# First layers of the last two tiles by Strassen's seven products, and one shared stage of second layers, in a retention and two feed-forward networks

## The chip, the cores and the metric

One core of a Trainium2 chip. The metric is the device time of one execution, in microseconds (us). TensorE (PE) multiplies matrices and adds up in PSUM, which has eight banks of 128x512 f32; VectorE (DVE), ScalarE (ACT) and GpSimd (POOL) do elementwise work; SyncE (SP) issues most DMAs. Each engine takes its instructions in the order in which they are written.

## The reference

```python
for t in range(S):
    state = gamma[None, :, None, None] * state + np.einsum('bhd,bhe->bhde', k[:, :, t], v[:, :, t])
    y[:, :, t] = scale * np.einsum('bhd,bhde->bhe', q[:, :, t], state)
...
h = x @ w_in
g = np.where(pos, h, np.where(neg, 0.0, (h + beta) ** 2 / (4.0 * beta)))
y1 = g @ w_out
...
a = x @ w1
b = x @ w2
h = a * b @ w3
return (h @ w_out).astype(np.float32)
```

Retention over 4 batches, 8 heads, 768 positions of 64; then the first network on 3072 tokens (512 to 2048 to 512), and the second (512 to 1024 twice, multiplied, to 1024, to 512). All inputs and outputs are f32.

## The kernel before

The 768 positions are cut in six chunks of 128 (c), so the tokens in six tiles (i) of 512. An f32 matrix is kept as two parts, a hi and the rest lo, and each product is three matmuls (hi hi, lo hi, hi lo): `split` makes the parts, hi by a cast on ACT, lo by a subtraction on DVE. Weights come from DRAM as raw words and pass a conversion of two ACT and four DVE operations (`convert`).

**The first network and the retention** are written by a planner. Its PE order is written by hand (the list `pe`), and the other engines' orders follow from costs and due times. `qk_ops` and `pv_ops` are the two attention pieces of a batch and chunk, with banks called pe or pa. `h_ops[i, f]` is a first layer's block f of 16 for tile i (bank hps, 12 matmuls), followed by Relu and Square on ACT and a max and min on DVE; `y_ops[i, f]` is the second layer's block f (banks y1acc, four at once, 12 matmuls). For tiles under LATE (0, 1 and 2) the first layers come ahead, beside the attention, and wait in DRAM (g_d). The last tile's blocks are written out by hand behind the plan, and beside them the weights of the second network are prepared: `prepare_ab` makes the seven operands of a unit and stores them in wab_d.

**The second network.** First w3 and the last matrix are multiplied together (`emit_w3o`, steps u = 0 to 15; `fetch_w3` reads blocks, `load_w3` splits one a step ahead; banks w3acc, result wc). Then come three pairs of tiles. A pair has eight units (f), and `emit_ab` does one: seven products of six matmuls in the order p1, p2, p6, p5, p7, p3, p4 (Strassen's scheme in its Winograd form), on the banks bank_a, bank_c and bank_b, of which ACT makes copies c. The eight sums c1 and c2 are multiplied elementwise to p and q. Between products stand output blocks of the unit before (`out_blocks`, oacc; four with three matmuls each). Behind the eighth unit come the output blocks of f = 6 and f = 7 for the first tile of the pair, the evacuation of their four banks (ost, ACT and DVE in turn), and a pass of 96 matmuls for the second tile in the same banks. The operands of the next pair (yop, seven for each half kb) are made of four sums t (`add_y`) and a split each (`split_y`), for kb = 0 in unit 6 and between the output blocks, for kb = 1 in the second tile's pass.

```python
                if more and f == 6:
                    add_y(i + 1, 0)
                    for _ in range(2):
                        split_y(*ahead.pop(0))
                    fetch_y1(i + 1, 1, range(2))
```

Units 0 to 7 come from wab_d or are made on the spot (unit 7), and later ones are read by `load_unit` two units ahead, 1792 KB each.

## Time and profile before

| | us |
|---|---|
| median of 3 runs (lowest, highest) | 1040.75 (1040.54, 1041.38) |
| profiled execution | 1037.49 |
| its span in the trace | 1035.7 |
| PE busy | 1016.9 |
| DVE busy | 566.1 |
| ACT busy | 437.5 |
| POOL busy | 93.1 |

The span runs from the first to the last instruction of the one profiled execution; its own time has 1.8 us more around it. Mean granted TensorE clock 0.998. Matmuls overlap, so the mean duration of one is longer than the step to the next one's start. In a timeline row the bracket tells how long the engine was idle before, and what ended it.

### The profile page before, as it was taken

What the parts mean: (1) busy time and instruction counts of PE and PEld (TensorE: products, weight loads), DVE (VectorE), ACT (ScalarE), POOL (GpSimd) and SP (SyncE); (2) the same over time, 40 slices, a digit from 0 to 9 for tenths busy, and PEclk for the clock granted to TensorE, in tenths of its full rate; (3) what the DMA queues carried; (4) which work ended last, traced back from release to release, by engine and by line L of the source; (5) the groups of instructions that cost most, each with busy time, mean ns of one, the idle gap of its engine ahead of it and who ended that gap; (6) DMA issues with size and microseconds to landing.
All of it is one profiled execution on the core that took longest, in us unless ns stands there. A gap on an engine that the chain in (4) does not pass through costs nothing.

```text
span 1035.7 us, 14337 instructions
## 1 busy us (share of the span) xinstructions
PE 1016.9 (98%) x5492; PEld 828.8 (80%) x5492; DVE 566.1 (55%) x847; ACT 437.5 (42%) x719; POOL 93.1 (9%) x121
## 2 busy tenths in 40 slices
PE   7799999999999999999999999999999999999998
PEld 5688878887788888888888887888878888888886
DVE  5988378724445666666536676633482434624340
ACT  3477457632233454455435555432341323322320
POOL 1212422211200001000000010000000000000000
PEclk9999999999999999999999999999999999999999
DMA  9997749939689977867638996344372435434402
GB/s 297 232 251 220 271 143 366 364 131 369 230 326 393 354 284 259 295 238 295 217 152 312 340 408 217 138 143 175 134 259 89 165 143 193 163 132 142 148 30 77
DMA packets 77384, 235.51 MB, mean 227 GB/s; under 512 B 9474, under 2 KB 9858, under 8 KB 71428
## 3 DMA queue, kind: packets, MB, share of 16 engines
q1 hardware_dynamic: 68576, 198.74, 54.9%
q0 software_dynamic: 8448, 35.66, 9.1%
q8 instruction: 43, 0.70, 0.3%
q10 hardware_dynamic: 292, 0.20, 0.1%
q14 instruction: 25, 0.20, 0.1%
HBM read 175.84 MB, written 58.72 MB: 226 GB/s over the span
## 4 chain that ended last, share of the span: by engine, by line
PE 86%; DMA 5%; issue 4%; DVE 2%; ACT 2%; POOL 0%; SPq 0%; DVEq 0%; POOLq 0%; ACTq 0%
PE bank_a L782 12%; PE y1acc L273 8%; PE y1acc L275 7%; PE y1acc L274 7%; PE hps L273 7%; PE hps L275 7%; PE hps L274 7%; PE bank_b L782 6%; PE oacc L823 4%; PE oacc L824 4%; PE oacc L825 4%; PE bank_c L782 3%; PE pa L513 2%; PE w3acc L275 1%; PE w3acc L274 1%
## 5 line engine op out<-in xcount | busy, mean ns | idle before, releaser
L273 PE MATMUL hps<-xh,win 128*128 128x512 f32 x384 | 152.0, 396 | 2.2 <-ACT xh L529 1.8
L273 PE MATMUL y1acc<-g,wo 128*128 128x512 f32 x384 | 151.6, 395 | 1.4 <-ACT g L269 1.4
L275 PE MATMUL hps<-xl,win 128*128 128x512 f32 x384 | 150.2, 391 | 0.0
L274 PE MATMUL hps<-xh,win 128*128 128x512 f32 x384 | 150.1, 391 | 0.0
L275 PE MATMUL y1acc<-g,wo 128*128 128x512 f32 x384 | 149.6, 390 | 0.0
L274 PE MATMUL y1acc<-g,wo 128*128 128x512 f32 x384 | 149.6, 390 | 0.0
L782 PE MATMUL bank_a<-yop,unit 128*128 128x512 f32 x576 | 146.0, 390 | 0.7 <-ACT c L797 0.6
L782 PEld LDWEIGHTS bank_a<-yop,unit 128*128 128x128 f32 x576 | 107.9, 188 | 24.0 <-ACT c L797 1.6
L587 ACT ACTIVATE r<-hps 128x512 f32<-128x512 f32 x81 | 48.4, 597 | 122.8 <-PE hps L275 119.4
L590 DVE SCALAR_TENSOR_TENSOR r<-hps,r 128x512 f32<-128x512 f32 x81 | 55.7, 688 | 81.2 <-ACT r L589 79.8
L273 PEld LDWEIGHTS hps<-xh,win 128*128 128x128 f32 x384 | 72.5, 189 | 19.9 <-ACT xh L529 2.3
L273 PEld LDWEIGHTS y1acc<-g,wo 128*128 128x128 f32 x384 | 72.0, 188 | 19.0 <-ACT g L269 1.8
L809 DVE TENSOR_TENSOR c<-bank_b,c 128x512 f32<-128x512 f32 x24 | 16.6, 692 | 128.0 <-PE bank_b L782 128.0
L275 PEld LDWEIGHTS hps<-xl,win 128*128 128x128 f32 x384 | 72.4, 188 | 16.1 <-DVE xl L530 0.9
L275 PEld LDWEIGHTS y1acc<-g,wo 128*128 128x128 f32 x384 | 72.1, 188 | 15.6 <-DVE g L270 0.4
L274 PEld LDWEIGHTS hps<-xh,win 128*128 128x128 f32 x384 | 72.5, 189 | 14.5
L274 PEld LDWEIGHTS y1acc<-g,wo 128*128 128x128 f32 x384 | 72.1, 188 | 14.4
L782 PE MATMUL bank_b<-yop,unit 128*128 128x512 f32 x288 | 73.1, 389 | 0.0
L782 PEld LDWEIGHTS bank_b<-yop,unit 128*128 128x128 f32 x288 | 54.1, 188 | 11.3
L589 ACT ACTIVATE r<-r 128x512 f32<-128x512 f32 x81 | 51.2, 632 | 2.6
L269 ACT CAST p<-c 128x512 fp32r<-128x512 f32 x24 | 14.9, 622 | 84.3 <-DVE c L814 84.3
L329 DVE TENSOR_TENSOR g<-g 128x512 fp32r<-128x512 f32 x48 | 33.1, 699 | 31.2 <-ACT g L327 31.2
(173 smaller groups left out, 1587.3 us busy)
## 6 DMA issues: line engine op xcount, KB each, us to landing
wo<-wo_d SPq DMA_DIRECT2D x80, 512.0 KB, 6.6
unit<-wab_d SPq DMA_DIRECT2D x23, 1024.0 KB, 4.8
unit<-wab_d SPq DMA_DIRECT2D x23, 768.0 KB, 4.2
g_d<-r POOLq DMA_DIRECT2D x48, 256.0 KB, 4.0
g<-g_d SPq DMA_DIRECT2D x48, 256.0 KB, 6.2
wo_d<-wo POOLq DMA_DIRECT2D x16, 512.0 KB, 6.0
raw<-in_w_dram SPq DMA_DIRECT2D x16, 512.0 KB, 6.7
raw<-in_w3t_dram SPq DMA_DIRECT2D x8, 1024.0 KB, 7.1
```

The costliest lines, as they stand in the source:

```text
L273: nc.tensor.matmul(out=ps, lhsT=lh, rhs=rh, start=first, stop=False)
L274: nc.tensor.matmul(out=ps, lhsT=ll, rhs=rh, start=False, stop=False)
L275: nc.tensor.matmul(out=ps, lhsT=lh, rhs=rl, start=False, stop=last)
L329: return plan.op("DVE", 0.7, lambda: nc.vector.tensor_tensor(out=dst.ap[:, 1, :], in0=at(), in1=dst.ap[:, 0, :], op=ALU.subtract), r=[src, ...
L513: nc.tensor.matmul(out=ps2.ap[64 * e:64 * e + 64, h, j * C:(j + 1) * C], lhsT=v_t[:, 2 * p + h, :] if own else old.ap[r, p, :], rhs=a_t[:, ...
L587: plan.op("ACT", 0.6, lambda: nc.scalar.activation(out=r.ap, in_=ps.ap, func=AF.Relu, bias=0.5, scale=0.5), r=[ps], w=[r])
L589: plan.op("ACT", 0.63, lambda: nc.scalar.activation(out=r.ap, in_=r.ap, func=AF.Square), w=[r])
L590: plan.op("DVE", 0.7, lambda: nc.vector.scalar_tensor_tensor(out=r.ap, in0=ps.ap, scalar=1.0, in1=r.ap, op0=ALU.max, op1=ALU.min), r=[ps], ...
L782: nc.tensor.matmul(out=ps, lhsT=x, rhs=z, start=first and kb + k == 0, stop=kb == 1 and k == 2, skip_group_check=True,)
L823: nc.tensor.matmul(out=ps, lhsT=lh, rhs=wh, start=(f == 0), stop=False)
L824: nc.tensor.matmul(out=ps, lhsT=lh, rhs=wl, start=False, stop=False)
L825: nc.tensor.matmul(out=ps, lhsT=ll, rhs=wh, start=False, stop=(f == NF2 - 1))
```

## The change

1. Tiles 4 and 5 (PAIR) do their first layers as the second network does its own: `plan_hu(n)` makes blocks 2n and 2n+1 for both tiles in seven products, on one bank h and the two banks of pa, with operands made by `plan_unit` and `plan_x_pair`. For the weights of it, the converted w_in blocks are stored in DRAM (win_d) behind their conversion, two of them from their parts by POOL (`keep_win`).
2. LATE is 4: tiles 0 to 3 have their g in DRAM. Tiles 3 and 2 share one stage of second layers: tile 3 takes two banks of h and the two of pa, tile 2 the four of acc, and each weight block is loaded once. Second layers of tile 4 lie between Strassen products, those of tile 5 end the plan; nothing is written by hand behind it.
3. Retention of chunks 4 and 5 lies beside the first layers of tile 3 and second layers of tile 1; `h_ops[0, 1]` stands ahead of `kv_ops[0]`, the mask's two multiplications are exchanged.
4. The second network's unit weights aren't prepared ahead. `prepare_unit` makes each of the 24 units from one 512 KB read: ACT and DVE split, POOL makes the four sums. w_out2 is converted in the plan's last stage, with one block of w3 (DIRECT).
5. `add_y` and all seven `split_y` of kb = 0 stand behind the eighth unit.

```diff
-LATE = 3
-EARLY_AB = 7
+LATE = 4
+PAIR = 4
+KEEP = 260.0
+DIRECT = 1
+FEW = 3
...
+            if n == 2:
+                d = win_kept[f] = win_kept[f + 1] = Val(None, None)
+                plan.op("SP", 0.45, lambda: nc.sync.dma_start(out=win_d[f // 2], in_=u.ap.bitcast(F32)),
+                        r=[u], w=[d], size=512)
...
+        if c >= PAIR:
+            for kb in range(2):
+                if (c, kb) not in xs:
+                    xs[c, kb] = Val("w", lambda: wpool.tile([P, 2, 512], F32, tag="w", name="xs"))
+                plan.op("ACT", 0.45, lambda kb=kb: nc.scalar.copy(
+                    out=xs[c, kb].ap[:, :, b * C:b * C + C], in_=got()[:, :, kb]), r=[ps2], part=[xs[c, kb]])
+        else:
+            split_x(b, c, ps2, got)
...
+    SUMS = ((3, 2, 3, ALU.add), (2, 0, 2, ALU.subtract), (0, 3, 0, ALU.subtract), (1, 1, 0, ALU.subtract))
...
+    def plan_unit(n):
+
+        u = Val("u", lambda: cpool.tile([P, 1024], F32, tag="u", name="u"))
+        uh = Val("xh", lambda: xpool.tile([P, NK, TT], F32R, tag="xh", name="unit"))
+        ul = Val("xl", lambda: xpool.tile([P, NK, TT], F32R, tag="xl", name="unit"))
+        plan.op("SP", 0.45, lambda: nc.sync.dma_start(out=u.ap, in_=win_d[n]),
+                r=[win_kept[2 * n], win_kept[2 * n + 1]], w=[u], size=512)
+
+        def halves(v, hi, lo, a, b):
+            done = Val(None, None)
+            plan.op("ACT", 0.18 + 0.00088 * (b - a), lambda: nc.scalar.copy(out=hi(), in_=u.ap[:, a:b]),
+                    r=[u], part=[v, done])
+            plan.op("DVE", 0.15 + 0.00106 * (b - a), lambda: nc.vector.tensor_tensor(
+                out=lo(), in0=u.ap[:, a:b], in1=hi(), op=ALU.subtract), r=[u, done], part=[v])
+
+        halves(uh, lambda: uh.ap[:, 0], lambda: uh.ap[:, 1], 0, 512)
+        halves(ul, lambda: ul.ap[:, 2, 0:256], lambda: ul.ap[:, 2, 256:512], 768, 1024)
+        for o, x, y, op in SUMS:
+            plan.op("DVE", 0.43, lambda o=o, x=x, y=y, op=op: nc.vector.tensor_tensor(
+                out=block(u.ap, o), in0=block(u.ap, x), in1=block(u.ap, y), op=op), w=[u])
+        halves(uh, lambda: uh.ap[:, 2], lambda: uh.ap[:, 3], 0, 512)
+        halves(ul, lambda: ul.ap[:, 0], lambda: ul.ap[:, 1], 512, 1024)
+        return uh, ul
...
+    def plan_hu(n):
+        uh, ul = plan_unit(n)
+        bank = Val("h", lambda: ps_h.tile([P, TT], F32, tag="h", name="bank"))
+        pair = Val("pa", lambda: psum["a"].tile([P, 2, 512], F32, tag="pa", name="banks"))
+        at = {"a": lambda: bank.ap, "x": lambda: pair.ap[:, 0], "y": lambda: pair.ap[:, 1]}
+        ops = hu_ops[n] = []
+
+        def product(name, where, first):
+            def fn():
+                w = views((uh.ap, ul.ap))[name]
+                for kb in range(2):
+                    x = xops[kb, name].ap
+                    lh, ll, rh, rl = w[:, 0, kb, :], w[:, 1, kb, :], x[:, 0, :], x[:, 1, :]
+                    for k, (l, r) in enumerate(((lh, rh), (ll, rh), (lh, rl))):
+                        nc.tensor.matmul(
+                            out=at[where](), lhsT=l, rhs=r, start=first and kb + k == 0,
+                            stop=kb == 1 and k == 2, skip_group_check=True,
+                        )
+
+            ops.append(plan.op("PE", 1.362, fn, r=[uh, ul, xops[0, name], xops[1, name]],
+                               w=[bank if where == "a" else pair]))
+
+        def copy(where):
+            c = Val("st", lambda: new_st("c"))
+            plan.op("ACT", 0.6, lambda: nc.scalar.copy(out=c.ap, in_=at[where]()),
+                    r=[bank if where == "a" else pair], w=[c])
+            return c
+
+        def gate(f, src, src_at, second):
...
+        product("p1", "a", True)
+        c1 = copy("a")
+        product("p2", "x", True)
+        plan.op("DVE", 0.7, lambda: nc.vector.tensor_tensor(
+            out=c1.ap, in0=pair.ap[:, 0], in1=c1.ap, op=ALU.add), r=[pair], w=[c1])
+        gate(2 * n, c1, lambda: c1.ap, False)
+        product("p6", "a", False)
+        c2 = copy("a")
+        product("p5", "y", True)
+        c5 = copy("y")
+        product("p7", "a", False)
+        c3 = copy("a")
+        product("p3", "y", False)
+        plan.op("DVE", 0.7, lambda: nc.vector.tensor_tensor(
+            out=c2.ap, in0=pair.ap[:, 1], in1=c2.ap, op=ALU.add), r=[pair], w=[c2])
+        gate(2 * n, c2, lambda: c2.ap, True)
+        plan.op("DVE", 0.7, lambda: nc.vector.tensor_tensor(
+            out=c3.ap, in0=c3.ap, in1=c5.ap, op=ALU.add), r=[c5], w=[c3])
+        gate(2 * n + 1, c3, lambda: c3.ap, True)
+        product("p4", "a", False)
+        gate(2 * n + 1, bank, lambda: bank.ap, False)
...
+        hs = [Val("h", lambda: ps_h.tile([P, TT], F32, tag="h", name="y1acc")) for _ in range(2)]
+        pair = Val("pa", lambda: psum["a"].tile([P, 2, 512], F32, tag="pa", name="y1acc"))
+        return [*((v, lambda v=v: v.ap) for v in hs), *((pair, lambda j=j: pair.ap[:, j]) for j in range(2))]
...
+        for n, i in enumerate(tiles):
+            if f == 0:
+                banks[i] = y_banks(i, n < len(tiles) - 1)
+            if i == PAIR + 1:
+                g = Val("wo", lambda: new_wo("g"))
+                plan_split(g, g_last[f // 2], (slice(None), f % 2))
+            else:
+                g, _ = gs.pop((i, f))
...
+    def load_unit(n):
+        u = wpool.tile([P, 1024], F32, tag="w", name="unit_w")
+        nc.sync.dma_start(out=u, in_=spill[("wab", n % NF2)])
+        arrived[("unit", n)] = u
+
+    def prepare_unit(n):
+
+        u = arrived.pop(("unit", n))
+        a, b = units_ahead = unit_tiles()
+        split(a[:, 0], a[:, 1], u[:, 0:512])
+        split(b[:, 2, 0:256], b[:, 2, 256:512], block(u, 3))
+        yield
+        for o, x, y, op in SUMS:
+            nc.gpsimd.tensor_tensor(out=block(u, o), in0=block(u, x), in1=block(u, y), op=op)
+        yield
+        split(a[:, 2], a[:, 3], u[:, 0:512])
+        yield
+        split(b[:, 0], b[:, 1], u[:, 512:1024])
+        units[n] = views(units_ahead)
...
-        pe += [h_ops[0, 0], kv_ops[0], qk_ops[0, 1], qk_ops[1, 1], pv_ops[0, 1], qk_ops[2, 1], pv_ops[1, 1],
-               h_ops[0, 1], qk_ops[3, 1], pv_ops[2, 1], pv_ops[3, 1]]
+        pe += [h_ops[0, 0], h_ops[0, 1], kv_ops[0], qk_ops[0, 1], qk_ops[1, 1], pv_ops[0, 1], qk_ops[2, 1],
+               pv_ops[1, 1], qk_ops[3, 1], pv_ops[2, 1], pv_ops[3, 1]]
...
+            if f < 10:
+                pe.append(y_ops[1, f + 4])
+                if f in (5, 9):
+                    pe.append(pieces.pop(0))
+        assert not pieces
+        pe += [y_ops[1, NF1 - 2], y_ops[1, NF1 - 1]]
...
+        few_jobs = len(pe)
+        lagging = [y_ops[2, NF1 - 2], y_ops[2, NF1 - 1], *(y_ops[PAIR, f] for f in range(NF1))]
+        for n in range(NF1 // 2):
+            for j, o in enumerate(hu_ops[n]):
+                pe.append(o)
+                if j in (1, 3):
+                    pe.append(lagging.pop(0))
+        end_jobs = len(pe)
+        pe += [y_ops[PAIR, NF1 - 2], y_ops[PAIR, NF1 - 1]]
+        last_jobs = len(pe)
+        pe += [y_ops[PAIR + 1, f] for f in range(NF1)]
...
+        raws = [(load_rows(w_out2[j], w_out2[j + 1]), finish_wo2(j), None) for j in range(0, NF2, 2)]
+        direct = [Val("wo", lambda: wpool.tile([P, 2, 512], F32, tag="wo", name="w3f", bufs=10)) for _ in range(DIRECT)]
+        for j in range(DIRECT):
+            raws.append((load_rows(w3t[j]), lambda u: None, direct[j]))
...
+        fetches = [u for h in range(2) for u in range(NF2 * h + DIRECT, NF2 * h + NF2)]
+        for n in range(0, len(fetches), 2):
+            fetch_w3(fetches[n:n + 2])
+            if n == 2:
+                fetch_y1(0, 0, range(4))
+        load_w3(0)
...
+            if u == 2 * NF2 - 2:
+                for _ in prepare_unit(0):
+                    pass
...
+        n_units = NF2 * (NTILE // 2)
         for i in range(NTILE // 2):
             more = i + 1 < NTILE // 2
-            ahead = y_of(i + 1)
             for f in range(NF2):
-                n = 8 * i + f
-                steps = prepare_ab(n + 1) if EARLY_AB <= n + 1 < NF2 else ()
+                n = NF2 * i + f
+                if 0 < n < n_units - 1:
+                    load_unit(n + 1)
+                steps = prepare_unit(n + 1) if n + 1 < n_units else iter(())
                 emit_ab(i, f, out_blocks(f - 1) if 0 < f < NF2 - 1 else (), steps)
-                if not EARLY_AB <= n + 2 < NF2 and n + 2 < 8 * (NTILE // 2):
-                    load_unit(n + 2)
-                if n + 4 in range(EARLY_AB, NF2):
-                    fetch_ab(n + 4)
+                for _ in steps:
+                    pass
                 if more and f == 5:
                     fetch_y1(i + 1, 0, range(4))
-                if more and f == 6:
-                    add_y(i + 1, 0)
-                    for _ in range(2):
-                        split_y(*ahead.pop(0))
-                    fetch_y1(i + 1, 1, range(2))
+            ahead = y_of(i + 1)
+            if more:
+                add_y(i + 1, 0)
             for x in out_blocks(NF2 - 2):
                 emit_out(*x)
             if more:
                 while ahead[0][1] == 0:
                     split_y(*ahead.pop(0))
-                fetch_y1(i + 1, 1, range(2, 4))
+                fetch_y1(i + 1, 1, range(4))
             for x in out_blocks(NF2 - 1):
                 emit_out(*x)
                 evac_out(2 * i, x[3], x[0])
```

**ACT at the join of two pairs.** Before: from the first copy of unit 7's bank_a to the copies (ost) of the first tile's banks; f_ and t__ are inputs and sums for yop.

```order
L797 COPY c_6556<-bank_a 128x512
L802 COPY c_6557<-bank_a 128x512
L804 COPY c_6559<-bank_b 128x512
L807 COPY c_6558<-bank_a 128x512
L269 CAST p<-c_6556 128x512
L269 CAST q<-c_6557 128x512
L269 CAST yop<-t__6537 128x512 x2
L269 CAST yop<-t__6538 128x512
L269 CAST yop<-f_6431 128x512
L269 CAST yop<-t__6538 128x512
L628 COPY ost<-oacc 128x512 x2
```

After, from unit 7's copy of bank_b on:

```order
L968 COPY c_6644<-bank_b 128x512
L971 COPY c_6643<-bank_a 128x512
L273 CAST unit<-unit_w 128x512 x2
L273 CAST p<-c_6641 128x512
L273 CAST q<-c_6642 128x512
L273 CAST yop<-f_6536 128x512
L273 CAST yop<-f_6540 128x512
L273 CAST yop<-t__6716 128x512 x2
L273 CAST yop<-t__6717 128x512
L273 CAST yop<-f_6542 128x512
L273 CAST yop<-t__6717 128x512
L832 COPY ost<-oacc 128x512 x2
```

Two casts of the next unit stand ahead of p and q, and all seven yop casts stand between q and the ost copies. Before there are five, and the two from f_ stood ahead of unit 7's first copy.

**DVE at the same join.** Before, from c1's multiplication of unit 7 on:

```order
L814 TENSOR_TENSOR c_6556<-bank_a,c_6556 128x512
L270 TENSOR_TENSOR p<-c_6556,p 128x512
L270 TENSOR_TENSOR q<-c_6557,q 128x512
L270 TENSOR_TENSOR yop<-t__6537,yop 128x512 x2
L270 TENSOR_TENSOR yop<-t__6538,yop 128x512
L270 TENSOR_TENSOR yop<-f_6431,yop 128x512
L270 TENSOR_TENSOR yop<-t__6538,yop 128x512
L630 COPY ost<-oacc 128x512 x2
```

After, from the same multiplication on, with the unit's subtraction ahead of it:

```order
L274 TENSOR_TENSOR unit<-unit_w,unit 128x512
L978 TENSOR_TENSOR c_6641<-bank_a,c_6641 128x512
L274 TENSOR_TENSOR unit<-unit_w,unit 128x512
L274 TENSOR_TENSOR p<-c_6641,p 128x512
L274 TENSOR_TENSOR q<-c_6642,q 128x512
L923 TENSOR_TENSOR t__6716<-f_6538,f_6536 128x512
L924 TENSOR_TENSOR t__6717<-f_6542,f_6538 128x512
L925 TENSOR_TENSOR t__6716<-f_6542,t__6716 128x512
L926 TENSOR_TENSOR t__6717<-f_6540,t__6716 128x512
L274 TENSOR_TENSOR yop<-f_6536,yop 128x512
L274 TENSOR_TENSOR yop<-f_6540,yop 128x512
L274 TENSOR_TENSOR yop<-t__6716,yop 128x512 x2
L274 TENSOR_TENSOR yop<-t__6717,yop 128x512
```

The four sums t have moved from unit 6 to behind q, ahead of the first yop subtraction.

**SP at the end of the second layers.** y_d is y1 in DRAM. Before, around the four stores of the last tile:

```order
L644 DMA f_5568<-y_d_82 128x512
L661 DMA w3f<-sp_w_4_202 128x512
L661 DMA w3f<-sp_w_5_203 128x512
L1023 DMA y_d_86<-y1st 128x512 x4
L661 DMA w3f<-sp_w_6_204 128x512
L661 DMA w3f<-sp_w_7_205 128x512
L644 DMA f_5748<-y_d_81 128x512
```

After:

```order
L800 DMA wo<-wo_d_102 128x1024
L365 DMA raw<-in_w3t_dram 128x2048
L839 DMA y_d_86<-y1st 128x512 x4
L857 DMA w3f<-sp_w_1_202 128x512
L857 DMA w3f<-sp_w_2_203 128x512
L857 DMA w3f<-sp_w_3_204 128x512
L857 DMA w3f<-sp_w_4_205 128x512
```

Each fetch serves one of the 16 steps u; before, those of the first 14 stand ahead of the four stores (the last two of them are shown), after, none does, and a raw read of w3's block 0 has their place.

**ACT at the second network's first unit.** Before, at the end of the w3 product:

```order
L269 CAST w3s<-w3f 128x512
L269 CAST yop<-f_5754 128x512
L269 CAST wc<-w3acc 128x512 x4
L269 CAST yop<-t__5805 128x512
L797 COPY c_5956<-bank_a 128x512
```

After:

```order
L273 CAST w3s<-w3f 128x512
L273 CAST yop<-f_5785 128x512
L273 CAST unit<-unit_w 128x512
L273 CAST unit<-unit_w 128x256
L273 CAST unit<-unit_w 128x512 x2
L273 CAST wc<-w3acc 128x512 x4
L273 CAST yop<-t__5836 128x512
L961 COPY c_5997<-bank_a 128x512
```

Four casts of unit 0 stand ahead of the four wc casts, and so ahead of c1's copy of bank_a.

## Rows read from the trace of the kernel before

**Rows 1.** The page's parts 1 and 2: busy time; PE in 40 slices.

```profile
PE 1016.9 (98%) x5492; PEld 828.8 (80%) x5492; DVE 566.1 (55%) x847; ACT 437.5 (42%) x719; POOL 93.1 (9%) x121
...
PE   7799999999999999999999999999999999999998
```

**Rows 2.** The page's part 5, a costly group: busy us, mean ns, idle before.

```profile
L273 PE MATMUL hps<-xh,win 128*128 128x512 f32 x384 | 152.0, 396 | 2.2 <-ACT xh L529 1.8
```

**Rows 3.** The chain that ended last, 600 to 680 us: start, us, what.

```profile
670.13 1.36 PE bank_a L782 x6
```

**Rows 4.** Waits of PE: waited for, us in total, times, longest us.

```profile
PE pe L513 <- DVE qk L482: 3.2, 1, 3.2
PE pe L513 <- DVE a L472: 2.5, 3, 1.5
...
PE pe L513 <- DVE sbd L537: 1.5, 1, 1.5
PE y1acc L273 <- ACT g L269: 1.4, 1, 1.4
PE bank_a L782 <- ACT c L797: 0.6, 1, 0.6
PE pe L513 <- DVE q L482: 0.5, 1, 0.5
PE oacc L823 <- ACT ost L628: 0.4, 2, 0.2
```

**Rows 5.** Windows of PE: us, busy (instructions), granted clock, DMA share, GB/s.

```profile
43.00:44.00 1.00, 1.00 (x15) 0.70 1.10 289
44.00:46.00 2.00, 2.00 (x5) 0.50 1.05 170
46.00:47.00 1.00, 1.00 (x4) 0.59 1.09 256
```

**Rows 6.** Timeline, end of the second layers: start, us, engine, line, operation.

```profile
623.33 0.50 PE L273 MATMUL y1acc<-g,wo 128*128 128x512 f32 x1 [1.38 <-ACT g L269]
...
626.43 2.46 SPq L1023 DMA_DIRECT2D y_d<-y1st  x4
626.45 0.39 PE L273 MATMUL w3acc<-wo,w3s 128*128 128x512 f32 x1
```

**Rows 7.** DMAs issued from 620 to 700 us: KB each, median us to landing.

```profile
f<-y_d SPq DMA_DIRECT2D x5, 256.0 KB, 2.7
...
w3f<-sp_w SPq DMA_DIRECT2D x4, 256.0 KB, 6.0
```

**Rows 8.** Timeline, first unit of the second network.

```profile
668.13 2.63 ACT L269 CAST wc<-w3acc 128x512 fp32r<-128x512 f32 x4 [2.26 <-PE w3acc L275]
...
671.53 0.59 ACT L797 COPY c<-bank_a 128x512 f32<-128x512 f32 x1 [0.25 <-PE bank_a L782]
```

**Rows 9.** POOL's groups: busy us, mean ns, idle before.

```profile
L482 POOL TENSOR_TENSOR q<-q,decay 128x512 f32<-128x512 f32 x16 | 22.2, 1385 | 204.4 <-PE pa L460 148.7 <-issue 53.6 <-PE pe L460 1.6
```

**Rows 10.** Timeline, first join of two pairs.

```profile
763.46 0.39 PE L823 MATMUL oacc<-wc,p 128*128 128x512 f32 x1
...
764.30 0.68 DVE L814 TENSOR_TENSOR c<-bank_a,c 128x512 f32<-128x512 f32 x1
...
765.02 0.62 ACT L269 CAST p<-c 128x512 fp32r<-128x512 f32 x1 [3.49 <-DVE c L814]
...
766.06 1.14 ACT L269 CAST yop<-t__6537 128x512 fp32r<-128x512 f32 x2
...
766.88 1.28 DVE L270 TENSOR_TENSOR yop<-t__6537,yop 128x512 fp32r<-128x512 f32 x2
...
768.67 1.10 ACT L628 COPY ost<-oacc 128x512 f32<-128x512 f32 x2
...
769.30 0.50 PE L823 MATMUL oacc<-wc,q 128*128 128x512 f32 x1 [0.20 <-ACT ost L628]
...
770.61 21.77 SPq L844 DMA_DIRECT2D out_dram<-ost  x8
```

More of the change, by code (lines that the diff above doesn't have):

```diff
@@ L261, in retention_then_two_ffns @@
     decay = const.tile([P, NP, C], F32, name="decay")
-    block = const.tile([P, NP, D], F32, name="block")
+    span = const.tile([P, NP, D], F32, name="span")
     small = const.tile([P, H + C], F32, name="small")
@@ L301, in convert @@
         for n, (cost, fn) in enumerate(load):
-            plan.op("SP", cost, lambda fn=fn: fn(raw.ap), part=[raw], size=s * 512 / len(load) * (1.6 if len(load) == 4 else 1.0), bound=bound, after=after)
+            plan.op("SP", cost, lambda fn=fn: fn(raw.ap), part=[raw], size=s * 512 / len(load) * (1.6 if len(load) == 4 else 1.0),
+                    bound=bound, after=after).floor = floor
         odd = lambda: raw.ap[:, 1::2]
@@ L335, in retention_then_two_ffns @@
     wo_kept = [None] * NF1
+    win_d = [dram.tile([P, 1024], F32, name=f"win_d{n}") for n in range(NF1 // 2)]
+    win_kept = {}
     def load_win(f, n):
@@ L537, in update @@
                 plan.op("DVE", 0.43, lambda: nc.vector.tensor_tensor(
-                    out=new.ap, in0=at(), in1=block, op=ALU.mult), r=[kv, blocks], w=[new])
+                    out=new.ap, in0=at(), in1=span, op=ALU.mult), r=[kv, blocks], w=[new])
             else:
@@ L543, in update @@
                 plan.op("DVE", 0.43, lambda: nc.vector.tensor_tensor(
-                    out=new.ap, in0=t.ap, in1=block, op=ALU.mult), r=[t, blocks], w=[new])
+                    out=new.ap, in0=t.ap, in1=span, op=ALU.mult), r=[t, blocks], w=[new])
             sbd[b] = new
@@ new lines, in keep_win @@
+    def keep_win(f, after, bound):
+        t, w = Val("st", lambda: new_st("win")), win[f]
+        d = win_kept[f] = Val(None, None)
+        plan.op("POOL", 1.36, lambda: nc.gpsimd.tensor_tensor(
+            out=t.ap, in0=w.ap[:, 0, :].bitcast(F32), in1=w.ap[:, 1, :].bitcast(F32), op=ALU.add),
+            r=[w], w=[t], after=after, bound=bound).floor = bound - 20.0
+        plan.op("POOL", 0.6, lambda: nc.gpsimd.dma_start(
+            out=win_d[f // 2][:, 512 * (f % 2):512 * (f % 2) + 512], in_=t.ap), r=[t], w=[d], size=256).floor = bound - 18.0
@@ new lines, in unit_tiles, with views @@
+    def unit_tiles():
+        return [xpool.tile([P, NK, TT], F32R, tag=t, name="unit") for t in ("xh", "xl")]
+    def views(tiles):
+        a, b = tiles
+        of = {"p1": (a, 0, 0), "p2": (a, 0, 1), "p6": (a, 2, 0), "p3": (a, 2, 1), "p7": (b, 0, 0), "p5": (b, 0, 1)}
+        found = {
+            name: t[:, i:i + 2, 256 * h:256 * h + 256].rearrange("p s (k w) -> p s k w", k=2)
+            for name, (t, i, h) in of.items()
+        }
+        found["p4"] = b[:, 2, :].rearrange("p (s k w) -> p s k w", s=2, k=2)
+        return found
@@ new lines, in retention_then_two_ffns, with y_banks @@
+    banks = {}
+    def y_banks(i, beside):
+        if not beside:
+            vals = [Val("acc", lambda: psum["acc"].tile([P, TT], F32, tag="acc", name="y1acc")) for _ in range(NK)]
+            return [(v, lambda v=v: v.ap) for v in vals]
+        hs = [Val("h", lambda: ps_h.tile([P, TT], F32, tag="h", name="y1acc")) for _ in range(2)]
+        pair = Val("pa", lambda: psum["a"].tile([P, 2, 512], F32, tag="pa", name="y1acc"))
+        return [*((v, lambda v=v: v.ap) for v in hs), *((pair, lambda j=j: pair.ap[:, j]) for j in range(2))]
@@ L754, in add_y @@
         if i:
-            t12, t34 = (late.tile([P, 2, 512], F32, tag="ws", name="t_", bufs=2) for _ in range(2))
+            t12, t34 = (late[1].tile([P, 2, 512], F32, tag="ws", name="t_", bufs=2) for _ in range(2))
             t1, t2, t3, t4 = t12[:, 0, :], t12[:, 1, :], t34[:, 0, :], t34[:, 1, :]
@@ L792, in emit_ab @@
         c1 = new_r("c1")
-        c2 = late.tile([P, TT], F32, tag="c2", name="c2", bufs=2)
+        c2 = late[1].tile([P, TT], F32, tag="c2", name="c2", bufs=2)
         c3 = new_r("c3")
@@ L909, in retention_then_two_ffns, with close_retention @@
             if x.tag == "pe" for u in x.users])
+        def close_retention():
+            retention.close()
+            late.append(ctx.enter_context(tc.tile_pool(name="late", bufs=1)))
+        closed = plan.op("POOL", 0.0, close_retention, after=of_retention)
         for o in plan.ops:
@@ L914, in retention_then_two_ffns @@
                 changed.after.append(o)
+            if any(x.tag == "g5" for x in o.vals):
+                o.deps.add(closed)
+                closed.after.append(o)
         pe = plan.pe
```

381 lines of the change are left out of this document (167 added, 214 removed).

## The prediction

> **What bounds the kernel now.** I read the engine table of the page first, then the costliest groups, TensorE's chain of waits by releaser, and last the timeline at the few places where TensorE stands still. The table says that TensorE (PE) is busy for 1016.9 of 1035.7 us, with VectorE (DVE) at 55% and ScalarE (ACT) at 42% [rows 1]. So the kernel is bounded by the number of matmuls, and what is left is some 19 us of idle PE. A saved matmul is not worth its own row: a 128x512 group shows a mean of 396 ns, but matmuls overlap [rows 2]. The price is the pitch: six of them take 1.36 us in the chain that ended last [rows 3], 0.227 us each. The waits give half of the idle time a name [rows 4]: 7.7 us for attention's banks (pe), 1.4 us ahead of the last piece of a second layer, 0.6 and twice 0.2 us at the joins between tile pairs. Outside the start and the end no slice of PE is under 0.9 [rows 1]. Hence whatever an edit takes from PE in a full stretch is a gain one for one, and each new wait on PE is a loss one for one; DVE and ACT count only where PE stands behind them.
>
> **Fewer products.** Tiles 4 and 5 did 2 x 16 x 12 = 384 matmuls in their first layers. Eight units of seven products of six are 336. The 48 that go are worth 48 x 0.227 = 10.9 us. The other counts stay: one stage of second layers for tiles 3 and 2 has the same matmuls as two.
>
> Does other work of the new stage lie on PE's path? A unit with its two second-layer pieces takes PE 42 x 0.227 + 24 x 0.227 = 15.0 us. ACT has four bank copies, eight Relu/Square passes, two g casts and 3.5 unit casts in it, 17.5 passes of about 0.62 us [rows 10], 10.9 us, and the three conversions left in the stage add under 1 us a unit. DVE has 9 operations of 512 columns on c and g, 3.5 on the unit and 4 sums of half width: about 14.5 at 0.69 us [rows 10], 10 us, and 1.5 us of conversions. Both fit with 3 us to spare, but one place is tight: p4 wants the copy of bank a that is made during p3's 1.36 us. Bounds: 0, and 0.5 us for each of eight units, 4 us. I take 1 us, nearer the end without a wait, since such a copy-under-a-product already runs in all the units of the second network without a row in the waits [rows 4].
>
> **Start.** The reordered first pieces put h 1 right behind h 0, ahead of the scaled queries and states that PE stood for: 3.2 us for qk, 1.5 for sbd, 0.5 for q [rows 4]. By the new order the last two attention blocks of chunk 1 still follow one another, each behind DVE's a, whose longest wait was 1.5 us [rows 4]; with the state ahead of it some 1.7 us each, 3.4 where 5.2 stood: a gain of 1.8 us. There is a second part. After the 3.2 us idle, which ended at 42.07, the granted clock went to 0.70, 0.50 and 0.59 [rows 5], so for some of 43 to 47 us PE was at the lower of its two levels (1.2 of 2.4 GHz); the shares missing to 1.00 sum to 0.3 + 1.0 + 0.4 = 1.7 us lost. Two waits of 1.7 us apart may keep the clock: behind the 1.4 us idle at 623.33 matmuls have 0.39 us, as everywhere [rows 6]. I take half, 0.8. Start: -2.6 us, bounds 0 and -6.9 (all of 5.2 and 1.7).
>
> **Into the w3 product.** Before, SP issues the fetches for the first 14 of the 16 steps ahead of the four stores of y1, and w3acc follows y1acc without a gap (626.45 behind the stores' start at 626.43) [rows 6]. Now only block 0 is at hand; the fetches of the others stand behind the four stores, and a store waits for its evacuation, the last one on ACT at about T+0.75 if T is the last matmul's end (the before's evacuations start within 1 us of their bank). ACT casts block 0 only behind that: u=0 begins at about T+1.8. The stores take 0.6 us each on SP (2.46 for four [rows 6]), so the fetch of block 1 goes out at about T+2, lands 2.7 us (256 KB from y1 in this stretch) to 6.0 us later (w3f itself) [rows 7], and is cast by T+5.4 to T+8.7, where u=0 has ended at T+4.5. In all 2.7 to 6 us of wait, and I take 4.1, less the 1.4 at 623.33 that goes: +2.7 us.
>
> **First unit of the second network.** Before, ACT made the last four wc casts (668.13, 2.63 us), one yop cast and then c1 at 671.53, and PE had no wait [rows 4, 8]. Now unit 0 is prepared there: three 512-column casts and a half, the last two of them behind four sums on GpSimd (POOL), stand ahead of the wc casts. The earlier ones wait for the end of u=14, E-2.7 us if E is the product's end; yop and 1.5 casts end at E-1.1, DVE's subtractions at about E-0.2. POOL has no 256-column sum in the trace; between half and all of its 512-column row of 1.39 us [rows 9] I take half, 2.8 us for four (5.5 at the other end). Then ACT: two casts to E+3.7, four wc casts to E+5.9, yop, c1 to E+7.0. p6 could go at E+2.7. Stall 4.3; 1.5 if the sums cost nothing, 7 at POOL's full row. I take +4.2 us.
>
> **Joins between tile pairs (two).** This is the largest loss. Before, two of the seven yop casts were made one unit earlier, with the t sums; measured from the first oacc of f=6 (763.46), c1 was multiplied at +0.84, p cast at +1.56, five yop casts followed at 0.52 us each, and the first ost copy began at +5.2; PE resumed at +5.84 with 0.20 us idle [rows 10]. Now a unit subtraction stands ahead of c1 (+0.6), and behind p and q come on DVE four t sums and on ACT seven yop casts, the third of which waits for t2. By the rows' durations: c1 at +1.45, ACT p to 2.8, q to 3.3; DVE p and q subtractions from 2.8 at 0.60 us pitch, t2 done at 5.9 (it depends on t1); yop 3 to 7 from 5.95 at 0.52, to 8.65; the first ost copy to 9.2. The 24 oacc matmuls end at 24 x 0.227 = 5.44. PE waits 3.75 us, 3.1 without the subtraction ahead; I take 3.6. Behind PE's wait is the whole second half of the outputs, then the next unit.
>
> Then, unit 9's (and 17's) load is one 512 KB read that SP issues behind the last ost store of that pass. Before, the eight stores held SP from 770.61 to 792.38 [rows 10], but units 8 and 9 had been read by then. The load now goes out about 1 us after the next pair begins, lands some 3.5 us later (2.7 to 6.0 [rows 7]), and its two casts stand ahead of c2's copy on ACT: p7 gets 0.8 us of wait (0 to 3). Two joins: 2 x (3.6 + 0.8) = 8.8, less the 0.6 + 0.4 that stood there [rows 4]: +7.7 us.
>
> **Clock after the new waits.** Three of them (4.3, 3.6, 3.6) are longer than the idle after which the clock fell. The fall cost 1.7 us there [rows 5]. That one followed a stretch of narrow attention matmuls, these follow dense work, so I count half of 5.1: +2.5 us, bounds 0 and 5.1. The Trainium skill (TensorE: Matmul & The Clock Gate, section HAM oscillation — how this bites in real kernels) says that a TensorE which repeatedly waits for data returns to half rate and restarts cold each time; by that rule all three fall and the sum is 2.6 us higher. The row at 43 to 46 us agrees with it, and no row of this case shows such a wait inside dense work.
>
> **Edits at nothing.** The eight extra win stores and loads, the retention pieces beside first layers, the in-plan conversions of w_out2 and the unit preparation in later units lie beside a full PE: a steady unit takes 12.2 us, and ACT 5.6, DVE 7.4 of it. If that cover were gone, the first to be late would be p and q casts, 0.6 us each.
>
> **Sum.** -10.9 + 1.0 - 2.6 + 2.7 + 4.2 + 7.7 + 2.5 = +4.6 us. The profiled execution took 1037.49 us (its span 1035.7 and 1.8 around it), which gives 1042.1; the runs' median is 1040.75, 0.3% above it, which gives 1045.4.
>
> **Rivals.**
> (1) The joins are covered: ACT reaches the first ost copy within 5.4 us of the first oacc. For it: all that is late is ACT's row, which has 42% load. Against: engines take their rows in order, and t2 cannot start before c1's multiplication. Without 2 x 3.6 us and two thirds of the clock's 2.5 behind them the time is 1036.5, faster. It decides from the point where these waits, clock included, lose 4.6 us of their 8.9, so about 2 us a join. Chance, with shorter waits at the other places that give 1030 to 1038.7: 0.33.
> (2) The new first-layer stage is bound by ACT and DVE: 3 us of slack a unit, used up if the tight copy and the queues lose 1.4 us in each of eight units: 11 us where I have 1, 1055. Against: nothing in the second network's units, which have the same chain, waits. Also here: the seven early win stores of 512 KB, 3.6 MB more in the first 110 us, make a first layer wait for its weights. 0.14.
> (3) The clock falls three times: 1048.0. It is inside the forecast's own range.
> (4) The saving itself fails because PE is not the limit there: PE has no gap in those stages, so I give this nothing beyond (2).
>
> **Numbers.** A measurement of this kernel can tell about 0.2%, 2.1 us, from no change. The forecast, waits as computed with or without the clock (own range 1041 to 1049), has 0.45; rival 1 0.33; rival 2 0.14; what falls between (the waits halve, the start gives more) 0.08. From these: faster by over 0.2% 0.34, within 0.2% 0.18 (0.08 and the forecast's low end), slower 0.48. The range reaches to rival 1's time and leaves out its fast end and most of rival 2: 1031 to 1051.
>
> **What would show it.** In the profile after: 48 fewer 128x512 rows; a PE wait of 2.7 to 6 us ahead of w3acc's first two blocks, its releaser w3s; one of about 4 us at the first unit's p6, released by ACT's c1; 3.6 us at the first oacc of each second half, released by ACT's ost; a granted clock of 0.5 behind some of them. The forecast is wrong if the rows at the joins are short, if the granted clock never leaves 1.00 and the start gains over 4 us, or if the waits of the new stage sum to more than 4 us.

## The result, and the profile after

The changed kernel takes 1055.22 us (median of 4 runs, 1053.04 to 1056.80) against 1040.64 of the kernel before on the same chips: the ratio is 1.0143, 95% interval 1.0118 to 1.0167. The forecast was slower, 1045.4, in a range to 1051. The direction was right and the size was not: 14.6 us where 4.6 were worked out, and 1055.22 is above the range.

The page of the kernel after, engine table and slices, to be read beside [rows 1]:

```profile
PE 1020.0 (97%) x5444; PEld 824.1 (78%) x5444; DVE 644.6 (61%) x957; ACT 500.8 (48%) x845; POOL 165.5 (16%) x221
...
PE   8899999999999999999999989899989999899998
...
PEclk8999999999999999999999999899999999899999
```

The 48 matmuls are gone (5492 to 5444), and yet PE is busy for 3 us more. That is the first sign that part of the loss is no wait: the same work ran slower. PE's slices have three dips in the second half, and at two of them its clock dips too.

PE's waits after, answering to [rows 4]:

```profile
PE oacc L987 <- ACT ost L832: 6.1, 2, 3.1
PE bank_a L946 <- ACT c L961: 4.3, 1, 4.3
PE w3acc L277 <- ACT w3s L273: 3.6, 2, 2.4
PE pe L530 <- DVE qk L499: 2.8, 2, 1.6
PE pe L530 <- DVE a L489: 2.3, 2, 1.7
...
PE bank_a L946 <- ACT c L966: 2.0, 2, 1.0
...
PE y1acc L277 <- DMA wo<-wo_d: 1.3, 1, 1.3
...
PE y1acc L277 <- ACT y1st L832: 0.9, 1, 0.9
```

The waits for ost, for c and for w3s are those of the forecast, place by place and releaser by releaser; the two at y1acc were not in it. What the list doesn't hold is in the windows (us, PE busy and instructions, granted clock, DMA share, GB/s):

```profile
20.00:30.00 10.00, 9.31 (x54) 0.76 1.07 281
...
620.00:630.00 10.00, 7.37 (x24) 0.83 0.96 324
670.00:680.00 10.00, 5.72 (x17) 0.67 0.18 54
...
770.00:780.00 10.00, 6.94 (x28) 1.00 0.28 87
...
900.00:910.00 10.00, 7.11 (x19) 0.66 0.60 211
```

The share missing to 1.00, times 10 us, is 1.7 us behind the wait for w3 block 1, 3.3 behind the first unit's wait, nothing behind the first join, 3.4 behind the second. Not all of that is lost, for the lower level (0.50, or 1.2 of 2.4 GHz) began within the wait at two of the places:

```profile
673.40:675.60 2.20, 0.00 (x0) 0.50 0.41 93
675.70:680.10 4.40, 4.40 (x10) 0.50 0.18 71
902.10:902.80 0.70, 0.00 (x0) 0.50 0.70 208
902.90:908.80 5.90, 5.90 (x14) 0.50 0.75 269
```

While PE works at 0.50, its matmuls start 0.43 us apart instead of 0.227, so about half of that busy time is lost: 2.2 us behind the first unit's wait and 3.0 behind the second join. With 1.7 in the w3 product, where PE was busy all through the fall, it makes 6.9 us. Before, one fall was seen, 1.7 us at 43 to 47 us [rows 5]. The kernel after has one in its start too (the row of 20 to 30 us).

Four marks that both traces have split the 17.5 us between the spans (1035.7 and 1053.2):

| from mark to mark | before, us | after, us | difference |
|---|---|---|---|
| start to tile 2's first hps (145.89; 146.08) | 145.9 | 146.1 | +0.2 |
| to the first w3acc (626.45; 618.26) | 480.6 | 472.2 | -8.4 |
| to the first bank_a of the pairs (669.97; 668.52) | 43.5 | 50.3 | +6.7 |
| to the end | 365.7 | 384.7 | +19.0 |

So the Strassen products did gain, and by the end of the w3 product after was still 1.5 us ahead. The loss stands in the second network, which the change only rearranges.

The timeline of its first unit, answering to [rows 8]:

```profile
668.32 3.18 POOL L904 TENSOR_TENSOR unit_w<-unit_w 128x256 f32<-128x256 f32 x4 [307.62 <-DVE unit L274]
...
671.54 1.14 ACT L273 CAST unit<-unit_w 128x512 fp32r<-128x512 f32 x2 [4.18 <-POOL unit_w L904]
...
672.58 2.04 ACT L273 CAST wc<-w3acc 128x512 fp32r<-128x512 f32 x4
...
675.01 0.62 ACT L961 COPY c<-bank_a 128x512 f32<-128x512 f32 x1
...
675.68 1.65 PE L946 MATMUL bank_a<-yop,unit 128*128 128x512 f32 x3 [4.28 <-ACT c L961]
```

POOL's four sums hold ACT for 4.18 us. Then come two unit casts, four wc casts, a yop, and only then the copy for which p6 waits. And the first join, answering to [rows 10]:

```profile
768.24 0.39 PE L987 MATMUL oacc<-wc,p 128*128 128x512 f32 x1
...
771.08 0.50 PE L987 MATMUL oacc<-wc,p 128*128 128x512 f32 x1
...
773.47 0.68 DVE L925 TENSOR_TENSOR t__6716<-f,t__6716 128x512 f32<-128x512 f32 x1
...
774.19 1.14 ACT L273 CAST yop<-t__6716 128x512 fp32r<-128x512 f32 x2 [1.60 <-DVE t__6716 L925]
...
776.80 1.06 ACT L832 COPY ost<-oacc 128x512 f32<-128x512 f32 x2
...
777.42 0.50 PE L987 MATMUL oacc<-wc,q 128*128 128x512 f32 x1 [3.06 <-ACT ost L832]
```

ACT waits 1.60 us for t2, casts five more yops, and the first ost copy ends 9.1 us behind the first oacc (9.2 were worked out). The first oacc of the second half starts 9.18 us behind it, against 5.84 before [rows 10].

### The profile page after: what moved, and what is told of

It reads as the page before. It is cut to its first block, busy times and chain, and to the rows that moved or that the text cites. A ratio compares the mean times of both kernels' runs of the same rounds, so it can differ in the third digit from the quotient of the medians.

```text
span 1053.2 us, 14552 instructions
## 1 busy us (share of the span) xinstructions
PE 1020.0 (97%) x5444; PEld 824.1 (78%) x5444; DVE 644.6 (61%) x957; ACT 500.8 (48%) x845; POOL 165.5 (16%) x221
## 3 DMA queue, kind: packets, MB, share of 16 engines
q1 hardware_dynamic: 63104, 163.34, 45.7%
## 4 chain that ended last, share of the span: by engine, by line
PE 85%; DMA 6%; ACT 3%; DVE 2%; SPq 1%; issue 1%; POOL 0%; DVEq 0%; POOLq 0%; ACTq 0%
PE bank_a L946 12%; PE y1acc L277 8%; PE y1acc L279 8%; PE y1acc L278 8%; PE bank_b L946 6%; PE hps L277 5%; PE hps L279 5%; PE hps L278 5%; PE oacc L987 4%; PE oacc L989 4%; PE oacc L988 4%; PE bank L731 4%; PE banks L731 3%; PE bank_c L946 3%; DMA raw<-in_w_in_dram 3%; PE pa L530 1%
## 5 line engine op out<-in xcount | busy, mean ns | idle before, releaser
L904 POOL TENSOR_TENSOR unit_w<-unit_w 128x256 f32<-128x256 f32 x96 | 70.9, 738 | 576.4 <-DVE unit L274 570.8
L946 PE MATMUL bank_a<-yop,unit 128*128 128x512 f32 x576 | 147.6, 393 | 6.3 <-ACT c L961 4.3
L277 PE MATMUL hps<-xh,win 128*128 128x512 f32 x256 | 102.9, 402 | 2.9 <-ACT xh L573 1.8
L279 PE MATMUL hps<-xl,win 128*128 128x512 f32 x256 | 100.6, 393 | 0.0
L278 PE MATMUL hps<-xh,win 128*128 128x512 f32 x256 | 100.6, 393 | 0.0
L613 ACT ACTIVATE r<-hps 128x512 f32<-128x512 f32 x64 | 38.2, 597 | 98.8 <-PE hps L279 97.3
L336 ACT CAST g<-g 128x512 fp32r<-128x512 f32 x80 | 48.9, 620 | 68.1 <-PE y1acc L279 59.0
L616 DVE SCALAR_TENSOR_TENSOR r<-hps,r 128x512 f32<-128x512 f32 x64 | 44.0, 688 | 53.5 <-ACT r L615 52.9
L338 DVE TENSOR_TENSOR g<-g 128x512 fp32r<-128x512 f32 x64 | 44.8, 713 | 32.9 <-ACT g L336 32.8
L274 DVE TENSOR_TENSOR unit<-unit_w,unit 128x512 fp32r<-128x512 f32 x96 | 57.2, 617 | 8.2 <-ACT unit L273 8.2
L277 PEld LDWEIGHTS hps<-xh,win 128*128 128x128 f32 x256 | 48.6, 190 | 16.8 <-DVE r L616 3.0
L621 POOL DMA_DIRECT2D g_d<-r x64 | 37.3, 583 | 138.1 <-DVE r L616 130.2
```

Of the source, the lines that this page charges most:

```text
L274: nc.vector.tensor_tensor(out=lo, in0=src, in1=hi, op=ALU.subtract)
L277: nc.tensor.matmul(out=ps, lhsT=lh, rhs=rh, start=first, stop=False)
L278: nc.tensor.matmul(out=ps, lhsT=ll, rhs=rh, start=False, stop=False)
L279: nc.tensor.matmul(out=ps, lhsT=lh, rhs=rl, start=False, stop=last)
L336: plan.op("ACT", 0.63, lambda: nc.scalar.copy(out=dst.ap[:, 0, :], in_=at()), r=[src], w=[dst, hi], bound=bound)
L338: return plan.op("DVE", 0.7, lambda: nc.vector.tensor_tensor(out=dst.ap[:, 1, :], in0=at(), in1=dst.ap[:, 0, :], op=ALU.subtract), r=[src, ...
```

## The experiments

Two theories were set against each other. **C**: what the forecast lacks are falls of PE's clock behind the new waits, each put at up to 3.4 us, the whole missing share. **W**: the waits and some slower work cost it, and the clock's rows are only how the records look. Each edit below is of the changed kernel. Gains are taken against its median of 1055.22 us. The experiments ran later, on three chips, where the kernel before took 1039.29 to 1039.80; reckoned by the ratio to it, a gain comes out up to 2 us different.

**Fill the waits, leave them in place.** Matmuls into an unused bank, 18 at the first unit and 13 at each join:

```diff
+        if i == 0 and f == 0:
+            t, y = w["p1"], yops[(0, 0, "p1")]
+            for _ in range(18):
+                nc.tensor.matmul(out=ps_p5, lhsT=t[:, 0, 0, :], rhs=y[:, 0, :], start=True, stop=True, skip_group_check=True)
         product("p6", bank, False)
...
+                spare = ps_h.tile([P, TT], F32, tag="h", name="spare")
+                for _ in range(13):
+                    nc.tensor.matmul(out=spare, lhsT=p1[0][:, 0, 0:P], rhs=wc[0][:, 0, :], start=True, stop=True)
```

> The changed kernel with 18 matmuls into an unused bank in the wait of the first unit and 13 in the wait of each of the two joins; nothing else waits less, so PE's successors start when they did. Theory C (the missing 10 us are falls of the granted clock behind the new waits: 3.4 us behind the first unit's, 3.4 us behind the second join's in the profiled run): granted clock 1.00 behind all three, 5 to 7 us faster, 1048 to 1050. Theory W (the waits themselves and slower work cost it, the clock shares are only how the records look): within 1.5 us of 1055, or slower by what the fill overruns.

Measured: 1050.76 us (1047.82 to 1051.37), 4.5 us faster by doing 44 matmuls more. Its windows:

```profile
670.00:680.00 10.00, 9.82 (x44) 1.00 0.18 52
...
770.00:780.00 10.00, 9.89 (x43) 1.00 0.41 152
...
900.00:910.00 10.00, 9.89 (x44) 1.00 0.54 184
```

p6 starts 7.16 us behind the first bank_a in both kernels, and the first oacc of a second half 9.18 to 9.20 us behind the join's first, so nothing waits less; only the clock stays at 1.00. That bears out C and speaks against W. The gain is 0.5 us under C's range because the range counted the missing share whole: the slow matmuls of these two places cost 5.2 us in the trace after (2.2 and 3.0), and from the first bank_a to the end the trace with filled waits takes 379.8 us instead of 384.7, 4.9 less.

**Evacuate first at the joins:**

```diff
-            if more:
-                add_y(i + 1, 0)
             for x in out_blocks(NF2 - 2):
                 emit_out(*x)
-            if more:
-                while ahead[0][1] == 0:
-                    split_y(*ahead.pop(0))
-                fetch_y1(i + 1, 1, range(4))
             for x in out_blocks(NF2 - 1):
                 emit_out(*x)
                 evac_out(2 * i, x[3], x[0])
             if more:
+                add_y(i + 1, 0)
+                while ahead[0][1] == 0:
+                    split_y(*ahead.pop(0))
+                fetch_y1(i + 1, 1, range(4))
                 add_y(i + 1, 1)
```

> The changed kernel, with the evacuation of the first tile's banks ahead of the t sums and yop casts at both joins. If ACT's row of casts holds PE there: the two waits of 3.06 us go, 6.3 us, and with theory C the 3.4 us of half clock behind the second, so 1045 to 1049. With theory W 1049. If the accumulators come free late for another reason (the data of out blocks): no change, 1055.

Measured: 1045.35 us (1044.06 to 1047.82), 9.9 faster. The waits for ost are gone from the list, and the first oacc of a second half starts 6.0 us behind the join's first instead of 9.18. The order of the rows was the cause there. The edit moves ACT's casts, DVE's sums and subtractions and SP's reads together, so it doesn't tell which of these rows alone would do. Twice 3.2 us and the 3.0 of the clock make 9.4 of the 9.9.

**Prepare unit 0 earlier:**

```diff
-            if u in (2 * NF2 - 5, 2 * NF2 - 3):
-                load_unit((u - 2 * NF2 + 5) // 2)
-            if u == 2 * NF2 - 2:
-                for _ in prepare_unit(0):
-                    pass
+            if u in (NF2, 2 * NF2 - 3):
+                load_unit(u // (2 * NF2 - 3))
+            if u == NF2 + 2:
+                first_unit = prepare_unit(0)
+            if u in range(NF2 + 2, NF2 + 6):
+                next(first_unit, None)
```

> The changed kernel, with unit 0 loaded and prepared in steps 8 to 13 of the w3 product instead of step 14. The wait of 4.28 us ahead of p6 goes; theory C adds the 3.4 us at half clock behind it: 1047 to 1048. Theory W: 1051. If the earlier casts delay the w3 blocks instead, some w3acc waits appear and less is gained.

Measured: 1047.81 us (1045.02 to 1048.34), 7.4 faster: the wait of 4.3 and a fall of the clock, as C has it. p6 starts 2.74 us behind the first bank_a instead of 7.16, and no fall follows; the first join has one here (770 to 780 us: 0.83) that after hasn't.

**Fetch w3's blocks ahead of the last stores.** The last tile's four y1 stores are held back until four fetches are issued:

```diff
+        if hold:
+            held.append((dst, st_at))
+            return
         plan.op("SP", 0.43, lambda: nc.sync.dma_start(out=dst, in_=st_at()), r=[done], use=[st], size=256)
...
             if n == 2:
+                for dst, st_at in held:
+                    nc.sync.dma_start(out=dst, in_=st_at())
                 fetch_y1(0, 0, range(4))
```

> The changed kernel, with the fetches of four w3 blocks ahead of the four last y1 stores on SP. The wait of 2.40 us ahead of the second step goes, that of 1.19 us ahead of the first stays (it is ACT's evacuations); theory C adds 1.7 us at half clock: 1051. Theory W: 1052.7. The w3 product's pitch of 0.234 us a matmul (0.227 elsewhere) should not change.

Measured: 1051.02 us (1048.81 to 1053.10), 4.2 faster; of w3acc's waits for ACT one of 1.4 us is left. From the first w3acc to the first bank_a it takes 45.9 us instead of 50.3. The step from one matmul's start to the next stayed at 0.234.

**Read units 9 and 17 earlier:**

```diff
-                if 0 < n < n_units - 1:
+                if 0 < n < n_units - 1 and f:
                     load_unit(n + 1)
...
             if more:
+                load_unit(NF2 * (i + 1) + 1)
```

> The changed kernel with units 9 and 17 read behind the first four output stores of a join instead of behind all eight. The waits for c's second copy of bank_a, twice 1.0 us, go: 1053.2, and no change of the granted clock's falls. If the copy is late for the casts themselves and not for the read: 1055.

Measured: 1050.64 us (1050.16 to 1051.14), 4.6 faster where 2.0 were expected. Both c waits are gone, so the read was late and not the casts. The rest is no effect of the edit that I can show. In its trace 1.6 us are gained ahead of the first w3acc already (616.63 against 618.26), where the edit changes nothing and the wait of 1.3 us for wo is not there. The falls of the clock differ both ways: shorter behind the second join (0.83 at 900 to 910 us, 0.66 in after), longer in the w3 product (0.66 at 620 to 630 us, 0.83 in after).

**The first pieces in the old order:**

```diff
-        pe += [h_ops[0, 0], h_ops[0, 1], kv_ops[0], qk_ops[0, 1], qk_ops[1, 1], pv_ops[0, 1], qk_ops[2, 1],
-               pv_ops[1, 1], qk_ops[3, 1], pv_ops[2, 1], pv_ops[3, 1]]
+        pe += [h_ops[0, 0], kv_ops[0], qk_ops[0, 1], qk_ops[1, 1], pv_ops[0, 1], qk_ops[2, 1], pv_ops[1, 1],
+               h_ops[0, 1], qk_ops[3, 1], pv_ops[2, 1], pv_ops[3, 1]]
```

> The changed kernel with the first pieces in the order of before (block 1 of tile 0's first layer behind the second value piece of chunk 1). My step said that the new order gains 1.8 us and keeps the clock: then 1057 to 1059. The profile says that the start gained nothing: 1054 to 1056, with a fall of the clock either near 20 us or near 44 us.

Measured: 1055.81 us (1054.15 to 1058.62), 0.6 slower, inside the spread, which is the second of the two expected times. The fall of the start lies at 40 to 50 us here (0.83), and none at 20 to 30 us; tile 2's first layer begins at 146.4 us, in after at 146.1.

**The pool of w3s on the other side of the memory:**

```diff
-        late.append(ctx.enter_context(tc.tile_pool(name="later", bufs=1, side="right")))
+        late.append(ctx.enter_context(tc.tile_pool(name="later", bufs=1)))
```

> The changed kernel with the pool of w3s on the other side of the memory. If the place of w3s makes the matmuls of the w3 product 0.234 us apart instead of 0.227: that pitch goes to 0.227 and 1.4 us are gained, 1053.8. If not: pitch 0.234, 1055.

Measured: 1055.13 us (1052.87 to 1058.84), no change that can be told. But the windows of the w3 product show one. After, and then with the other side:

```profile
630.00:660.00 30.00, 30.00 (x130) 1.00 0.34 113
```

```profile
630.00:660.00 30.00, 30.00 (x134) 1.00 0.32 107
```

More matmuls fit in the same 30 us at the same clock; from start to start they are 0.234 us apart after and 0.227 with the edit. From the first w3acc to the first bank_a it takes 48.7 us, 1.5 less than in after.

**All four repairs and the early read together:**

> The changed kernel with the evacuations first at the joins, unit 0 early, the fetches ahead of the stores, and units 9 and 17 read behind the first four output stores. The single edits gave 9.9, 7.4 and 4.2 us; with 2.0 us for the two c waits of 1.0: 1031.7, faster than the kernel before by 8 us. By theory C the granted clock is 1.00 from 40 us on. If the edits share a loss (one wait moved from one place to the next), the sum is not reached: 1036 to 1040.

Measured: 1031.71 us (1029.83 to 1036.27), ratio to the kernel before 0.9929 (0.9910 to 0.9949). That is 23.5 us faster than after and the expected time to the tenth, which is luck: the expectation put 2.0 us for the early read, and with the 4.6 which that edit gave alone the single gains sum to 26.1. From the first bank_a to the end it takes 365.9 us, the kernel before 365.7: in the second network's pairs nothing of the loss is left. Windows behind places where waits were:

```profile
620.00:630.00 10.00, 10.00 (x45) 1.00 0.99 346
...
670.00:680.00 10.00, 10.00 (x43) 1.00 0.17 52
890.00:900.00 10.00, 10.00 (x45) 1.00 0.15 54
```

**The same with the pool on the other side:**

> The kernel with the four edits at the joins, the first unit and the w3 blocks, and the pool of w3s on the other side. The pitch of 0.227 in the w3 product, seen with that edit alone, gives 1.4 us where no fall of the clock hides it: 1030.3. If the pitch hangs on something else: 0.234 and 1031.7.

Measured: 1030.74 us (1028.15 to 1033.65), ratio 0.9918 (0.9898 to 0.9938), the fastest median of all. The w3 product takes 44.2 us where all repairs alone need 45.7, so the 1.5 us are there; the two medians are 1.0 apart, and their intervals overlap.

**And with the first pieces in the old order:**

> The same kernel with the first pieces in the order of before. My step said that the new order gains 1.8 us, 2.6 with the clock: then 1032 to 1033. What the runs so far show (tile 2's first layer begins between 145.5 and 146.8 us in all of them, with or without a fall of the clock ahead of it): the start up to there is bounded by more than PE, and the time is within 1 us of the kernel with the new order.

Measured: 1032.29 us (1030.04 to 1033.15), 1.5 slower than with the new order, with ranges that overlap. The median is in the first expectation's range and 0.5 us outside the second's, which is too little to tell them apart. In the traces tile 2's first layer begins 0.7 us later than with the new order (147.6 against 146.9).

## Why the prediction was wrong

By its own steps, beside what the trace after shows:

| step | forecast, us | measured, us |
|---|---|---|
| 48 matmuls, new stage | -10.9 + 1.0 | -8.4 from 146 us to w3acc, with waits of 1.3 (wo) and 0.9 (y1st); the new stage's own 0.2 |
| start | -2.6 | +0.2 to 146 us |
| into the w3 product, in all | 4.1 | 1.19 + 0.23 + 2.40 + 0.23 |
| first unit | 4.2 | 4.28 |
| a join, first oacc of the second half | 3.6, at 9.2 behind the first oacc | 3.06, 3.06, at 9.18 |
| a join, c ahead of p7 | 0.8 | 1.02, 0.97 |
| clock behind the new waits | +2.5 | 1.7 + 2.2 + 0 + 3.0 |
| pitch of the w3 product | - | 1.5 |
| unit preparation in later units | 0 | 1.4 at the first output blocks of the three pairs |

**The step that failed is the clock.** The forecast took one fall of 1.7 us as the price, halved it because dense work stood around the waits, and counted none for the w3 wait. In the runs dense work is no such protection. Over all traces that keep a wait, the clock fell behind the first unit's wait in six of six, behind the second join's in six of six, behind that for w3 block 1 in seven of seven, and behind the first join's in one of six. The filled waits show that without the idle time there is no fall. One fall cost up to 3.0 us. In after they came to 6.9 us, 4.4 more than the sum had. So a wait of 3 to 4 us in this kernel costs some two thirds more than the trace's wait says: the two joins gave 9.9 us for 6.1 us of waiting, the first unit 7.4 for 4.3. The Trainium skill (TensorE: Matmul & The Clock Gate, section HAM oscillation — how this bites in real kernels) describes a kernel whose PE starts cold again after each wait for data; the forecast quoted that rule and gave it half weight. The trace after agrees with the rule at three of its four waits, and not at the first join, where the clock stayed at 1.00.

**The start failed too, by 2.8 us.** The idle ahead of attention's banks did shrink, from 7.7 us [rows 4] to 5.1. But tile 2's first layer began at 146.1 instead of 145.9, and the clock, which the shorter waits were to keep, fell all the same (0.76 at 20 to 30 us). In all ten experiments it began between 145.5 and 147.6, whether the clock had fallen ahead of it, for a shorter or a longer stretch, or not at all. So the stretch up to there isn't bounded by PE alone, and a PE wait that goes there isn't a gain one for one. The first paragraph of the prediction had made the start an exception; the sum booked its waits one for one all the same. The chain that ended last names what lies behind them. Before, and then after, 8 to 82 us (start, us, what):

```profile
24.43 6.30 DMA raw<-in_w_in_dram
30.75 5.59 DMA vk<-in_k_dram
36.38 1.24 DVE u L316
37.64 1.95 DVE u L318
...
41.32 0.61 DVE qk L482
```

```profile
25.27 7.13 DMA qk<-in_kT_dram
32.42 10.35 DMA raw<-in_w_in_dram
...
49.50 0.68 DVE r L616
```

In both it runs through reads of inputs, one behind the other, up to 36 and to 43 us, and then through work on ACT and DVE, conversions of w_in among it. The 3.2 us of PE that ended at 42.07 stood at the end of such a chain, and another order of PE's pieces alone would not shorten that. No run changed the reads, so this is read from the traces and not tested.

**What held.** The repairs took the waits away one by one, but for those of 1.2 to 1.4 us at the start of the w3 product, and each was there for the reason given: rows taken in order on ACT and SP, with nothing late but what stood ahead. The 10.9 us of the products follow from their count and pitch; the stretch from tile 2's first layer to w3acc, where they lie, is 8.4 us shorter in after and 9.3 with all repairs. All repairs together are 7.6 us faster than the kernel before on the same chip. The joins took what was worked out (9.18 us to the first oacc of the second half). The wait's row there shows 0.5 us less, since PE's idle time began 6.1 us behind the first oacc (777.42 - 3.06 - 768.24) and not 5.4, as f=7's blocks started late themselves (771.08 is 2.84 us on, against the 2.72 of twelve matmuls) and the last matmul's own end counts as busy.

Rival 3, the clock falling behind each wait, was nearest: at its three waits the falls cost 5.2 us where it had 5.1. But its 1048.0 is 7.2 us short, as what else failed is not in it. Rival 1, covered joins, is what the evacuate-first edit makes of them.

**What is left.** The span's difference has 12.9 us beyond the sum. 4.4 of clock, 2.8 of the start, 1.5 of pitch and the 1.7 by which the stretch to w3acc missed its terms (-8.4, where -10.9 + 1.0 and 0.2 less of wait at its end were counted) make 10.4. Another 1.4 us the forecast had among its edits at nothing. At the end of the first unit of each pair a unit subtraction on DVE stands ahead of c1's multiplication, so p comes late for the first output blocks:

```profile
685.53 0.68 DVE L274 TENSOR_TENSOR unit<-unit_w,unit 128x512 fp32r<-128x512 f32 x1
...
686.13 0.68 DVE L978 TENSOR_TENSOR c<-bank_a,c 128x512 f32<-128x512 f32 x1
...
686.85 0.62 ACT L273 CAST p<-c 128x512 fp32r<-128x512 f32 x1 [3.06 <-DVE c L978]
...
687.52 0.50 PE L987 MATMUL oacc<-wc,p 128*128 128x512 f32 x1
...
688.25 0.50 PE L989 MATMUL oacc<-wc,p 128*128 128x512 f32 x1
```

Four matmuls start 0.33 to 0.39 us apart there instead of 0.23, and the list of waits shows none of it. The last 1.1 us was not followed up; single runs differ by more.

## What to carry to other kernels

Price a new wait on TensorE by more than its length: in a kernel that is dense in matmuls, look at the granted clock behind every new wait, with the share of the fall in which PE works, and if the wait can't go, see whether spare matmuls in it pay. When work is moved to the place where it is needed, look at what stands behind it in the in-order row of each engine, evacuations first: an order that costs nothing to change gave 9.9 us here. And before an idle stretch is booked as a gain, check that what follows it starts earlier when it shrinks.
